# Units of the first token group in another order, nine idle products inside the first scores, first wides behind chunk 1

## The chip, the cores and the metric

The kernel runs on one core of one Trainium2 chip. TensorE (PE), VectorE (DVE), ScalarE (ACT), GpSimd (POOL) and SyncE (SP, here only a queue that issues DMAs) each work through their own instructions in order and wait for one another by semaphores. The metric is the device time of one execution in microseconds. The kernel before has a median of 972.02 us over 3 runs (971.38 to 975.17).

## The reference, cut to what matters

Three layers run one behind the other: a gated linear attention, a bilinear layer, and a mixture of eight experts of which each token takes two.

```python
for t in range(S):                                   # B=4, H=8, S=768, D=48
    state = alpha[:, :, t, :, None] * state + np.einsum('bhd,bhe->bhde', k[:, :, t], v[:, :, t])
    y[:, :, t] = np.einsum('bhd,bhde->bhe', q[:, :, t], state)
x = y.transpose(0, 2, 1, 3).reshape(3072, 384)
a = x @ w1;  b = x @ w2                              # 384 -> 1024
x = ((a * b) @ w3) @ w_out                           # 1024 -> 1024 -> 384
top2 = the two greatest of x @ w_gate + log1p(exp(x @ w_noise)) * noise
out[mask] += top2_w * (np.maximum(x[mask] @ e_w1[e], 0) @ e_w2[e])   # for each of 8 experts
```

The weights of the bilinear layer arrive as 64-bit floats, which the kernel converts itself. The large products run on pairs of 16-bit halves, three products for one.

## The kernel before, in words

The 3072 tokens are cut into eight groups of 384, each group into three chunks of 128 tokens. The attention works chunk by chunk: `prep_decay` and `prep_qk` (per pair of heads) turn alpha, q and k so that heads lie along the partitions and scale q and k by running products of alpha; `scores` (chunk j) multiplies them, copies the result out of PSUM (ACT, then a mask on POOL, for the first three chunks; DVE for the others); `ktok` turns k back; `mix` adds what the carried state gives and the scores times v, takes the greatest exponent of the result (a square on ACT, three short steps on DVE) and splits it into two 16-bit halves (ACT the high one, DVE the low one); `state` updates the carried state, which the next chunk's `mix` needs; `xturn` turns the split output into `xT`, copied out by ACT (L396). With `xT` of a group, `wide` forms a tile of `a` or `b` (nine products of 128 weights by the group's tokens), and `narrow` the product with the fused w3·w_out.

In the first 110 us there is a second stream of work: the weights of the bilinear layer are converted by `to_float32` and `split`, one block of 128 rows at a time, 36 blocks. Each costs DVE a shift (L410), ACT a copy of 16-bit words (L411), DVE a merge (L412), ACT the high half (L174) and DVE the low half (L178).

PE's instructions stand in the order in which the program is written (`manual_schedule`); those of DVE, ACT, POOL and SP are put in order by a scheduler, which works from its own costs. The writing is done by the loop at the end of `body`: it draws units from `att_units`, each with a cost, and until the third chunk of the first group is turned (`MS = 2`) it follows each unit either by a `wide` on the first chunk's 128 tokens (once chunk 0 is turned and six of the blocks are converted) or by three products of no use on a tile of zeros (`warm`, 128x512, L1161). Behind that point it interleaves units of attention with `mix_units` (the wides on the remaining 256 tokens, then full groups, then `narrow`) by a running sum of costs. `fetch` on SP's queue reads the weight blocks; its last four reads before `load(1)`, which reads alpha, q, k, v of the second group, wait until blocks 3 to 6 are converted, since they reuse their rooms.

Of the kernel before, what the change touches and what calls it, by code (L numbers as in the profile page):

```python
# [19 lines left out]
B, H, S, D = 4, 8, 768, 48  # L20
P = 128
# [4 lines left out]
NK = DM // P  # L26
# [16 lines left out]
RF = 5  # L43
RG = 6
WB = 12
WU = 3
WP = 3
TA = 30
CS = 1.5
# [29 lines left out]
def body(ctx, tc, q, k, v, alpha, mw1, mw2, mw3, mwo, wg, wn, noise, ew1, ew2, out, dbg=None):  # L79
# [208 lines left out]
    def scores(j):  # L288
        r, cols = cut(j)
        scs = [bank(NP, P) for _ in range(2)]  # L290
        for h in range(H):
            rows = slice(64 * (h % 2), 64 * (h % 2) + D)
            nc.tensor.matmul(scs[h % 2][:, h // 2, :], r["Kt"][rows, h // 2, cols], r["Qt"][rows, h // 2, cols],
                             start=True, stop=True)
        SM[j] = []
        for s in range(2):
            if j // TG in SCL:
                sf = late.tile([P, NP, P], F32, name="sf")
                sm = late.tile([P, 2, NP, P], F16, name="sm16", bufs=4)
                nc.vector.tensor_tensor(sf, scs[s], CSL[j // TG][:, None, :].to_broadcast([P, NP, P]), OP.mult)  # L300
                split(sf, sm[:, 0], sm[:, 1], engine=nc.gpsimd)
                SM[j].append(sm)
                continue
            sm = ap_.tile([P, NP, P], F32, name="sm", bufs=3)
            if j in AFF:
                nc.scalar.activation(sm, scs[s], AF.Copy)
                nc.gpsimd.affine_select(out=sm, in_=sm, pattern=[[0, NP], [1, P]], compare_op=OP.is_ge, fill=0.0,
                                        base=0, channel_multiplier=-1)
            else:
                nc.vector.tensor_tensor(sm, scs[s], causal[:, None, :].to_broadcast([P, NP, P]), OP.mult)  # L310
            SM[j].append(sm)
        if j // TG in SCL:
            VH[j] = late.tile([P, 2, H, D], F16, name="vh")
            split(VT[j], VH[j][:, 0], VH[j][:, 1], SCL[j // TG][:, 1:2])
# [74 lines left out]
    def xturn(j):  # L389
        ys = YS.pop(j)  # L390
        if j % TG == 0:
            XT[j // TG] = xp.tile([P, 2 * NK, G], F16, name="xT")
        xt = bank(2 * NK, P, dt=F16)
        for kk in range(2 * NK):
            nc.tensor.transpose(xt[:, kk, :], ys[:, kk // NK, kk % NK * P:(kk % NK + 1) * P], ident16)
        nc.scalar.activation(XT[j // TG][:, :, j % TG * P:(j % TG + 1) * P], xt, AF.Copy)  # L396
# [38 lines left out]
    nconv = 0  # L435
# [80 lines left out]
    def wide(g, f, i, c1=G):  # L516

        xT = XT[g]
        fs = slice(f * P, (f + 1) * P)
        c0 = GS.get((g, f, i), 0)  # L520
        GS[g, f, i] = c1
        cs, n = slice(c0, c1), c1 - c0
        pm = bank(n)
        for kk in range(NK):
            nc.tensor.matmul(pm, wab[i][0][:, kk, fs], xT[:, kk, cs], start=kk == 0, stop=False)  # L525
            nc.tensor.matmul(pm, wab[i][0][:, kk, fs], xT[:, NK + kk, cs], start=False, stop=False)  # L526
            nc.tensor.matmul(pm, wab[i][1][:, kk, fs], xT[:, kk, cs], start=False, stop=kk == NK - 1)  # L527
        a = gp.tile([P, G], F32, name=f"ab{i}")[:, :n]
        nc.scalar.activation(a, pm, AF.Copy, scale=SG if i == 0 else 1.0)  # L529
        AB[i] = a  # L530
        if i:
            a = AB[0]
            nc.vector.tensor_tensor(a, AB[1], a, OP.mult)
            if c0 == 0:
                GS[g, f] = [gp.tile([P, G], F16, name=x, bufs=10) for x in ("gh", "gl")]
            gh, gl = GS[g, f]
            split(a, gh[:, cs], gl[:, cs], engine=nc.gpsimd if g == 0 and f in PGL else None)
# [151 lines left out]
    def unit(c, f, *a):  # L689
        return c, (lambda: f(*a))  # L690

    def att_units():
        yield unit(0.0, prep_open, 0)
        for pr in range(NP):
            yield unit(0.33, prep_decay, 0, pr)
            if pr:
                yield unit(0.66, prep_qk, 0, pr - 1)
        yield unit(0.66, prep_qk, 0, NP - 1)
        yield unit(1.7, scores, 0)
        yield unit(0.44, ktok, 0)  # L700
        yield unit(1.7, scores, 1)
        yield unit(2.55, mix, 0)
        yield unit(0.44, ktok, 1)
        yield unit(0.75, state, 0)
        yield 0.34, (lambda: (xturn(0), done.add(0)))
        yield unit(0.0, loads_of_1)
        yield unit(1.7, scores, 2)
        yield unit(2.55, mix, 1)
        yield unit(0.44, ktok, 2)
        yield unit(0.75, state, 1)  # L710
        yield 0.34, (lambda: (xturn(1), done.add(1)))
        yield unit(0.0, prep_open, 1)
        yield unit(0.0, norms, 1)
        yield unit(0.33, prep_decay, 1, 0)
        yield unit(2.55, mix, 2)
        yield unit(0.33, prep_decay, 1, 1)
        yield 0.34, (lambda: (xturn(2), done.add(2)))
        yield unit(0.66, prep_qk, 1, 0)
        yield unit(0.33, prep_decay, 1, 2)
        yield unit(0.66, prep_qk, 1, 1)  # L720
        yield unit(0.33, prep_decay, 1, 3)
        yield unit(0.66, prep_qk, 1, 2)
        yield unit(0.66, prep_qk, 1, 3)
        yield unit(0.0, scales_of, 1)
        yield unit(0.0, load, 2)
        yield unit(0.0, tables)
        yield unit(0.75, state, 2)
        yield unit(1.7, scores, 3)
        yield unit(0.44, ktok, 3)
        for j in range(TG, NG * TG):  # L730
            st, cc = divmod(j, TG)
            more = st + 1 < NG
            if j + 1 < NG * TG:
                yield unit(1.7, scores, j + 1)
            if more and cc == 0:
                yield unit(0.0, prep_open, st + 1)
                yield unit(0.0, norms, st + 1)
                yield unit(0.33, prep_decay, st + 1, 0)
                yield unit(0.33, prep_decay, st + 1, 1)
            yield unit(2.55, mix, j)  # L740
            if more and cc == 0:
                yield unit(0.66, prep_qk, st + 1, 0)
                yield unit(0.33, prep_decay, st + 1, 2)
            if more and cc == 1:
                yield unit(0.66, prep_qk, st + 1, 2)
            if j + 1 < NG * TG:
                yield unit(0.44, ktok, j + 1)
            yield unit(0.75, state, j)
            if more and cc == 0:
                yield unit(0.66, prep_qk, st + 1, 1)  # L750
                yield unit(0.33, prep_decay, st + 1, 3)
            if more and cc == 1:
                yield unit(0.66, prep_qk, st + 1, 3)
                yield unit(0.0, scales_of, st + 1)
                if st + 2 < NG:
                    yield unit(0.0, load, st + 2)
            yield 0.34, (lambda j=j: (xturn(j), done.add(j)))
# [405 lines left out]
    done, ready = set(), set()  # L1163
# [3 lines left out]
    with tc.manual_schedule(engines={mybir.EngineType.PE}):  # L1167
        M = iter(mix_units())
        nxt = next(M)
        ta = tm = t0 = 0.0  # L1170
        warm(WB)
        for c, f in att_units():
            turned = set(done)
            f()
            ready |= turned
            ta += c
            if MS not in done:
                t0 = ta
                dve = [i for i in nc.cur_bb.bb.instructions[-40:] if i.engine == mybir.EngineType.DVE]
                marks += dve[-1:]  # L1180
                if marks:
                    with tc.issue_after(marks[max(0, len(marks) - LAG)]):
                        convert(int(CR * (ta - CS)))
                if c and 0 in done and nconv >= 2 * NK and pieces:
                    wide(0, *pieces.pop(0), P)
                elif c:
                    warm(WP if ta < 4.1 else WU)
                continue
            while nxt is not None and nxt[2] in ready | {0} and tm < RATIO * (min(ta, TK) - t0) + R2 * max(ta - TK, 0.0):
                nxt[1]()  # L1190
                tm += nxt[0]
                nxt = next(M, None)
        att.close()
        open_experts()
        early = iter(EARLY)
        while nxt is not None:
            nxt[1]()
            if nxt[0]:
                prepare(next(early, 1))
            nxt = next(M, None)  # L1200
        li = experts()
# [33 lines left out]
```

## Time and profile before

| | us |
|---|---|
| median of 3 runs | 972.02 |
| profiled execution, own time | 978.31 |
| its span, first to last instruction | 976.6 |
| PE busy in the span | 924.2 |
| DVE busy | 616.1 |
| ACT busy | 457.8 |
| mean granted clock of TensorE | 0.973 |

The profiled execution lies 6.3 us above the median. A row of the timeline gives the start, the busy time, the engine, the line and the operation with output and inputs, its shape and count; in brackets stands how long the engine sat idle before it and what ended that. A row of a window gives its length, then for PE, weight loads, DVE, ACT and POOL the busy time and count, then the granted clock as a share of 2.4 GHz, and the DMA share. Float32 products count twice (x16 for eight). A busy time of one row can overlap the start of the next by about 0.1 us.

### The profile page before, as it was taken

Reading aid. Unit: us, or ns where it says so; the run is one execution under the profiler, and the core shown is the slowest. Engines: PE = TensorE matmul, PEld = TensorE weight load, DVE = VectorE, ACT = ScalarE, POOL = GpSimd, SP = SyncE. Lnnn points to the kernel's source line nnn. Section 1 sums busy time; section 2 is a strip of 40 time slices with the busy share of each in tenths; the row PEclk is TensorE's granted clock in tenths of the full one; section 3 lists DMA queues with packets and bytes.
Section 4 is the critical chain, followed back from the end, with each engine's and each line's share of the span. In section 5 each row is a group of like instructions: output and inputs, shape, how many; then the busy total and the mean of one; then the engine's idle time right before and its main releaser. Section 6 shows DMA issues by size and latency. Waiting matters only on the chain. (4 is left out here: it accounts for less than half of the span.)

```text
span 976.6 us, 17652 instructions
## 1 busy us (share of the span) xinstructions
PE 924.2 (95%) x6823; PEld 607.8 (62%) x6823; DVE 616.1 (63%) x1697; ACT 457.8 (47%) x916; POOL 254.0 (26%) x246
## 2 busy tenths in 40 slices
PE   7889999999899998999999989999999999999996
PEld 4777777777666675666655445654656565656564
DVE  6698878576778697686768736626354454545320
ACT  3876665363565746555446424324243343334321
POOL 1121110004041311204052061433333333333313
PEclk9798899999999999999999989999999999999998
DMA  9886571334805224000234264874658575656313
GB/s 242 224 163 109 162 195 53 63 52 145 187 3 96 27 66 58 25 2 26 68 102 127 87 129 139 138 174 104 167 89 163 102 178 118 161 124 157 41 13 46
DMA packets 189269, 105.54 MB, mean 108 GB/s; under 512 B 156912, under 2 KB 174912, under 8 KB 189184
## 3 DMA queue, kind: packets, MB, share of 16 engines
q1 hardware_dynamic: 172624, 68.04, 31.5%
q0 software_dynamic: 16560, 36.37, 17.3%
q8 instruction: 54, 0.88, 0.4%
q14 instruction: 31, 0.25, 0.1%
HBM read 73.06 MB, written 20.31 MB: 96 GB/s over the span
## 5 line engine op out<-in xcount | busy, mean ns | idle before, releaser
L904 DVE SCALAR_TENSOR_TENSOR hl<-ps,hh 128x512 f16<-128x512 f32 (+1 forms) x128 | 74.9, 587 | 110.9 <-ACT hh L903 110.9
L934 POOL DMA_INDIRECT out_dram<-ysb,mt x56 | 88.3, 1576 | 210.3 <-ACT ysb L933 91.3
L900 PE MATMUL ps<-xT,eh 128*128 128x320 f16 (+1 forms) x384 | 132.0, 344 | 4.5 <-DMA xT<-xg 4.5
L901 PE MATMUL ps<-xT,eh 128*128 128x320 f16 (+1 forms) x384 | 131.9, 344 | 0.0
L902 PE MATMUL ps<-xT,el 128*128 128x320 f16 (+1 forms) x384 | 131.7, 343 | 0.0
L912 PE MATMUL ps<-eh,hl 128*128 128x384 f16 x384 | 125.2, 326 | 0.0
L911 PE MATMUL ps<-el,hh 128*128 128x384 f16 x384 | 125.2, 326 | 0.0
L910 PE MATMUL ps<-eh,hh 128*128 128x384 f16 x384 | 125.2, 326 | 0.0
L903 ACT ACTIVATE hh<-ps 128x512 f16<-128x512 f32 (+1 forms) x128 | 65.9, 516 | 113.6 <-PE ps L902 112.5
L933 ACT ACTIVATE ysb<-ps,wv 128x384 f32<-128x384 f32 (+1 forms) x56 | 32.5, 580 | 151.9 <-PE ps L912 75.2
L178 DVE SCALAR_TENSOR_TENSOR el<-es,esc,eh 128x512 f16<-128x512 f32 (+1 forms) x80 | 67.0, 856 | 46.4 <-ACT eh L174 45.1
L679 POOL DMA_INDIRECT table<-md,ad x48 | 49.3, 1028 | 162.7 <-DVE ad L676 130.4
L888 POOL DMA_INDIRECT xg<-x2s,mt x56 | 56.4, 1008 | 57.8 <-DMA mt<-table 37.6
L176 POOL TENSOR_TENSOR sm<-sf,sm 128x512 f16<-128x512 f32 x24 | 28.4, 1203 | 161.1 <-ACT sm L174 161.1
L529 ACT ACTIVATE ab<-ps 128x384 f32<-128x384 f32 (+2 forms) x136 | 61.4, 465 | 17.0 <-PE ps L527 15.5
L525 PE MATMUL ps<-xT,w1h 128*128 128x384 f16 (+2 forms) x204 | 65.7, 323 | 2.0 <-ACT ab L529 1.5
L525 PE MATMUL ps<-xT,w0h 128*128 128x384 f16 (+2 forms) x204 | 65.4, 322 | 1.1 <-ACT xT L396 1.1
L549 PE MATMUL ps<-Wh,gh 128*128 128x400 f16 x192 | 63.9, 333 | 2.2 <-ACT gh L174 2.2
L527 PE MATMUL ps<-xT,w1l 128*128 128x384 f16 (+2 forms) x204 | 65.8, 323 | 0.0
L526 PE MATMUL ps<-xT,w1h 128*128 128x384 f16 (+2 forms) x204 | 65.7, 323 | 0.0
L526 PE MATMUL ps<-xT,w0h 128*128 128x384 f16 (+2 forms) x204 | 65.4, 322 | 0.0
L527 PE MATMUL ps<-xT,w0l 128*128 128x384 f16 (+2 forms) x204 | 65.3, 321 | 0.0
(285 smaller groups left out, 2080.6 us busy)
## 6 DMA issues: line engine op xcount, KB each, us to landing
es<-in_moe_w_dram SPq DMA_DIRECT2D x32, 768.0 KB, 4.8
s<-in_moe_w_dram POOLq DMA_DIRECT2D x16, 512.0 KB, 4.3
out_dram<-zero POOLq DMA_DIRECT2D x5, 960.0 KB, 9.4
v<-in_v_dram SPq DMA_DIRECT2D x24, 192.0 KB, 3.6
x2s<-xr SPq DMA_DIRECT2D x24, 192.0 KB, 1.9
pad<-in_alpha_dram SPq DMA_DIRECT2D x21, 192.0 KB, 4.3
pad<-in_q_dram SPq DMA_DIRECT2D x21, 192.0 KB, 4.8
pad<-in_k_dram SPq DMA_DIRECT2D x21, 192.0 KB, 5.0
```

Of the source, the lines that this page charges most:

```text
L178: nc.vector.scalar_tensor_tensor(lo, src, scale, hi, op0=OP.mult, op1=OP.subtract)
L525: nc.tensor.matmul(pm, wab[i][0][:, kk, fs], xT[:, kk, cs], start=kk == 0, stop=False)
L526: nc.tensor.matmul(pm, wab[i][0][:, kk, fs], xT[:, NK + kk, cs], start=False, stop=False)
L527: nc.tensor.matmul(pm, wab[i][1][:, kk, fs], xT[:, kk, cs], start=False, stop=kk == NK - 1)
L900: nc.tensor.matmul(pm, w1h[:, kk, fs], xT[:, kk, :n], start=kk == 0, stop=False)
L901: nc.tensor.matmul(pm, w1h[:, kk, fs], xT[:, NK + kk, :n], start=False, stop=False)
L902: nc.tensor.matmul(pm, w1l[:, kk, fs], xT[:, kk, :n], start=False, stop=kk == NK - 1)
L904: nc.vector.scalar_tensor_tensor(hl[:, f], pm, 0.0, hh[:, f], op0=OP.max, op1=OP.subtract)
L910: nc.tensor.matmul(py[:n], hh[:, f, ts], w2h[:, f], start=f == 0, stop=False)
L911: nc.tensor.matmul(py[:n], hh[:, f, ts], w2l[:, f], start=False, stop=False)
L912: nc.tensor.matmul(py[:n], hl[:, f, ts], w2h[:, f], start=False, stop=f == NF - 1)
L934: i = queued(lambda: nc.gpsimd.indirect_dma_start(out=out, out_offset=bass.IndirectOffsetOnAxis(ap=mt[:n, t, 0:1].bitcast(U32), axis=0), i ...
```

## The change

The units of the first three chunks are written in another order (`scores` of chunk 1 and both `ktok` before the first `mix`, `scores` of chunk 2 before the first `xturn`, two more units of the second group's preparation before the third `xturn`). Three products of no use follow only the units of the preparation (cost sum under 4.1). Nine of them stand inside the scores of chunk 0, ahead of the last two heads. The eight wides on the first chunk come in pairs, from the turn of chunk 1 on.

```diff
-WU = 3
+W0 = 9
...
         for h in range(H):
             rows = slice(64 * (h % 2), 64 * (h % 2) + D)
+            if j == 0 and h == H - 2:
+                warm(W0)
             nc.tensor.matmul(scs[h % 2][:, h // 2, :], r["Kt"][rows, h // 2, cols], r["Qt"][rows, h // 2, cols],
...
         yield unit(1.7, scores, 0)
+        yield unit(1.7, scores, 1)
         yield unit(0.44, ktok, 0)
-        yield unit(1.7, scores, 1)
+        yield unit(0.44, ktok, 1)
         yield unit(2.55, mix, 0)
-        yield unit(0.44, ktok, 1)
         yield unit(0.75, state, 0)
+        yield unit(1.7, scores, 2)
         yield 0.34, (lambda: (xturn(0), done.add(0)))
         yield unit(0.0, loads_of_1)
-        yield unit(1.7, scores, 2)
         yield unit(2.55, mix, 1)
...
         yield unit(0.33, prep_decay, 1, 0)
+        yield unit(0.33, prep_decay, 1, 1)
         yield unit(2.55, mix, 2)
-        yield unit(0.33, prep_decay, 1, 1)
+        yield unit(0.66, prep_qk, 1, 0)
         yield 0.34, (lambda: (xturn(2), done.add(2)))
-        yield unit(0.66, prep_qk, 1, 0)
...
-                if c and 0 in done and nconv >= 2 * NK and pieces:
-                    wide(0, *pieces.pop(0), P)
-                elif c:
-                    warm(WP if ta < 4.1 else WU)
+                if c and ta < 4.1:
+                    warm(WP)
+                elif c and 1 in done:
+                    for piece in pieces[:2]:
+                        wide(0, *piece, P)
+                    del pieces[:2]
                 continue
```

In the changed program lines behind the scores stand two lower (L411 is L413, L529 is L531). On PE, behind the preparation of the first group, a piece of the program before reads as follows: `mix` of chunk 0, three useless products (each with its weight load), `ktok` of chunk 1.

```order
L343 MATMUL ps<-v,sm 128x48 x8
L1161 LDWEIGHTS ident_67
L1161 MATMUL ps<-idle,ident_67 128x512
L1161 LDWEIGHTS ident_67
L1161 MATMUL ps<-idle,ident_67 128x512
L1161 LDWEIGHTS ident_67
L1161 MATMUL ps<-idle,ident_67 128x512
L322 MATMUL ps<-ident,Kt 128x128 x4
```

In the changed program PE has there, from the last of the nine products inside the scores on (L295 is scores, L324 ktok, L345 mix, L364 state, L397 xturn):

```order
L1163 LDWEIGHTS ident_67
L1163 MATMUL ps<-idle,ident_67 128x512
L295 MATMUL ps<-Qt,Kt 128x128 x10
L324 MATMUL ps<-ident,Kt 128x128 x8
L345 MATMUL ps<-v,sm 128x48 x8
L364 MATMUL ps<-v,ks 112x96 x4
L295 MATMUL ps<-Qt,Kt 128x128 x8
L397 LDWEIGHTS ys
L397 MATMUL ps<-ident_67,ys 128x128
```

The scores of chunk 2 stand ahead of the turn of chunk 0, no useless product is left between these units, and the 21 that stood behind the preparation (seven triples) are replaced by the nine.

On ACT, at the first scores, before: the word copy of a block (L411), its high half (L174), the two copies of the scores (L306), two more word copies with `ktok`'s copy between them.

```order
L411 ACTIVATE w1h<-w1h 128x512
L174 ACTIVATE w0h<-s_319 128x512
L306 ACTIVATE sm<-ps 128x512 x2
L411 ACTIVATE w1l<-w1l 128x512
L324 ACTIVATE ks<-ps 128x512
L411 ACTIVATE x_142<-x_142 128x512
```

In the changed program:

```order
L413 ACTIVATE w1h<-w1h 128x512
L174 ACTIVATE w0h<-s_319 128x512
L413 ACTIVATE w1l<-w1l 128x512
L413 ACTIVATE x_142<-x_142 128x512
L308 ACTIVATE sm<-ps 128x512 x2
L174 ACTIVATE w0h<-s_369 128x512
```

Both word copies have moved ahead of the copies of the first scores.

On ACT, at the third chunk of the first group, before (L350 is the square that follows `mix` of chunk 2, L529 takes a wide out of PSUM, L222 the turned alpha, `gh` is the high half of a product `a*b`, the last row the copy of the turned chunk into `xT`):

```order
L174 ACTIVATE gh<-ab_648 128x128
L411 ACTIVATE s_145<-s_145 128x512
L174 ACTIVATE w1h<-s_632 128x512
L350 ACTIVATE ys,xsc<-ps 128x384
L411 ACTIVATE xT<-xT 128x384
L529 ACTIVATE ab_749<-ps 128x128
L222 ACTIVATE A_760<-ps 128x3x128
L174 ACTIVATE ys<-ps,xsc 128x384
L174 ACTIVATE w1h<-s_727 128x512
L396 ACTIVATE xT<-ps 128x6x128
```

In the changed program (L352 is the square, L398 the copy):

```order
L174 ACTIVATE gh<-ab_676 128x128
L352 ACTIVATE ys,xsc<-ps 128x384
L531 ACTIVATE ab_738<-ps 128x128
L413 ACTIVATE s_145<-s_145 128x512
L413 ACTIVATE xT<-xT 128x384
L174 ACTIVATE ys<-ps,xsc 128x384
L174 ACTIVATE w1h<-s_716 128x512
L174 ACTIVATE woh<-s_722 128x384
L531 ACTIVATE ab_750<-ps 128x128
L413 ACTIVATE xT<-xT 128x384
L398 ACTIVATE xT<-ps 128x6x128
```

The square stands right behind a high half of the third product `a*b`; between it and the copy there are three word copies instead of one. That product is made on DVE, and DVE's order before it has both preparations of the second group's first two pairs:

```order
L229 SCALAR_TENSOR_TENSOR Gx<-A_611,Bend 128x384
L228 MEMSET A_655 128x4
L230 RECIPROCAL Bst_117<-Gx 128x3
L232 TENSOR_TENSOR Ae<-sm_615,Gx 128x3
L229 SCALAR_TENSOR_TENSOR Gx<-A_655,Bend 128x384
L231 SCALAR_TENSOR_TENSOR A<-A_611,Bst_117 128x384
L230 RECIPROCAL Bst_118<-Gx 128x3
L232 TENSOR_TENSOR Ae<-sm_659,Gx 128x3
L535 TENSOR_TENSOR ab_676<-ab_688,ab_676 128x128
```

Before, the third such product stood ahead of the first step of such a preparation (L227):

```order
L373 TENSOR_TENSOR Zs_119<-ps,Zs_120 48x4x48
L410 TENSOR_SCALAR s_632<-s_144 128x512
L374 TENSOR_TENSOR Zs_119<-Zs_119,Ae 48x4x48
L533 TENSOR_TENSOR ab_648<-ab_668,ab_648 128x128
L227 COPY sm_687<-A_683 128x3
```

Three scans (L229, L231) have moved ahead of a product for which ACT's queue waits.

## Rows read from the trace of the kernel before

**Rows 1.** Page, busy us of each engine, share of the span, instructions
```profile
PE 924.2 (95%) x6823; PEld 607.8 (62%) x6823; DVE 616.1 (63%) x1697; ACT 457.8 (47%) x916; POOL 254.0 (26%) x246
```

**Rows 2.** Windows: length, busy us (count) of PE, PEld, DVE, ACT, POOL; clock; DMA
```profile
25.00:50.00 25.00, 22.13 (x161) 19.02 (x160) 16.38 (x33) 20.26 (x34) 4.04 (x8) 0.71 0.83 218
50.00:75.00 25.00, 20.28 (x187) 17.37 (x184) 24.17 (x60) 17.53 (x38) 5.35 (x8) 0.93 0.92 163
...
23.30:53.10 29.80, 25.92 (x196) 21.89 (x194) 19.50 (x41) 25.06 (x45) 6.32 (x11) 0.73 0.89 221
53.10:75.30 22.20, 18.18 (x152) 15.46 (x152) 21.41 (x54) 14.43 (x30) 4.16 (x6) 0.92 0.88 160
```

**Rows 3.** Windows cut where the granted clock changes, and one stretch of full clock
```profile
22.30:25.60 3.30, 3.18 (x12) 1.95 (x13) 1.06 (x4) 2.35 (x4) 1.22 (x2) 0.50 1.09 343
...
36.00:49.50 13.50, 12.97 (x86) 12.49 (x86) 7.38 (x17) 8.76 (x16) 1.82 (x3) 0.50 0.74 151
...
56.50:59.70 3.20, 3.20 (x17) 2.06 (x17) 2.87 (x10) 2.73 (x7) 0.00 (x0) 0.50 1.03 249
...
77.00:83.60 6.60, 6.60 (x40) 5.66 (x39) 5.66 (x14) 4.40 (x10) 0.67 (x1) 0.50 0.77 87
83.70:110.90 27.20, 26.35 (x221) 21.74 (x218) 25.05 (x68) 21.06 (x46) 3.66 (x7) 1.00 0.46 121
```

**Rows 4.** Timeline of PE at the second group's first scores: start, busy, count [idle before]
```profile
75.38 0.49 PE L293 MATMUL ps<-Qt,Kt 48*128 48x128 f32 x4 [0.65 <-DVE Kt L240]
```

**Rows 5.** Timeline of PE through the first group
```profile
22.42 0.80 PE L293 MATMUL ps<-Qt,Kt 48*128 48x128 f32 x4 [3.18 <-DVE Qt L240]
...
27.95 1.88 PE L343 MATMUL ps<-v,sm 128*128 128x48 f32 x16
...
31.40 0.94 PE L362 MATMUL ps<-v,ks 128*112 128x96 f32 x8
...
37.58 2.08 PE L293 MATMUL ps<-Qt,Kt 48*128 48x128 f32 x16
...
42.29 3.54 PE L343 MATMUL ps<-v,sm 128*128 128x48 f32 x16
...
46.58 1.06 PE L322 MATMUL ps<-ident,Kt 128*128 128x128 f32 x4
...
48.40 1.52 PE L362 MATMUL ps<-v,ks 128*112 128x96 f32 x8
...
50.26 0.50 PE L395 MATMUL ps<-ident,ys 128*128 128x128 f16 x6
...
53.87 1.10 PE L332 MATMUL ps<-Zs,Qt 112*128 112x96 f32 x8 [1.78 <-DVE Zs L374]
...
61.61 0.27 PE L525 MATMUL ps<-xT,w0h 128*128 128x256 f16 x1 [0.24 <-ACT xT L396]
```

**Rows 6.** Windows of the useless products alone (L1161): busy (count) of PE, PEld; clock
```profile
23.10:34.00 10.90, 5.72 (x18) 1.78 (x18) 0.88 1.01 324
58.30:60.00 1.70, 1.49 (x3) 0.30 (x2) 0.57 1.03 298
```

**Rows 7.** Timeline of ACT through the first group
```profile
23.25 1.09 ACT L306 ACTIVATE sm<-ps 128x512 f32<-128x512 f32 x2 [2.97 <-PE ps L293]
...
45.50 0.60 ACT L306 ACTIVATE sm<-ps 128x512 f32<-128x512 f32 x1 [3.54 <-PE ps L343]
...
56.97 0.49 ACT L350 ACTIVATE ys<-ps 128x384 f16<-128x384 f32 x1 [0.48 <-PE ps L343]
...
60.75 0.81 ACT L396 ACTIVATE xT<-ps 128x768 f16<-128x768 f16 x1 [0.57 <-PE ps L395]
```

**Rows 8.** Groups of ACT, 22 to 62 us: count, busy us, mean ns
```profile
L411 ACT ACTIVATE s<-s 128x512 uint16<-128x512 uint16 x3 | 4.0, 1342 | 0.0
```

**Rows 9.** Groups of DVE, 23.3 to 75.3 us
```profile
L229 DVE TENSOR_TENSOR_SCAN Gx<-A,Bend 128x384 f32<-128x384 f32 x4 | 4.2, 1040 | 0.0
```

**Rows 10.** Timeline of SP's queue: first read of the second group
```profile
40.43 3.62 SPq L186 DMA_DIRECT2D pad<-in_alpha_dram  x3
```

## The prediction

> **What bounds the kernel now.** I read the page first, then windows over the span, then windows cut where the clock changes, then the timelines of PE, ACT and DVE side by side for the first 110 us. PE is busy 95% of the span [rows 1], so time is won only where PE idles, runs slowly or does useless work. The change touches the first group, and there PE is not alone: from 25 to 50 us it is busy 22.13 of 25 at a mean clock of 0.71, ACT 20.26; from 50 to 75 PE is busy 20.28 and DVE 24.17 [rows 2]. The reader is to see three things. The chain of scores, mask, mix, square, split and turn runs through four engines, each of which also converts weights in between. PE is at half clock from 22.3 to 25.6, 36 to 49.5 and 56.5 to 59.7 [rows 3], each time after a gap or after short products. And the stage ends on DVE: the second group's first scores wait for the scaled q and k, the last of them until 75.38 [rows 4], while DVE has been busy 21.41 of 22.2 us [rows 2]. Behind them PE runs 77 to 83.6 at half clock without a gap, then is busy 26.35 of 27.2 us at full clock, DVE 25.05 [rows 3]. So three things decide: when DVE has that last k, how much PE has done by then, and at which clock PE goes on.
>
> **The change part by part.** All times are of the profiled execution, 978.31 us (span 976.6), which lies 6.29 above the median of 972.02; differences are carried over to the median as they are.
>
> *Nine products inside the scores.* Before the last two heads PE waits 3.18 us for q [rows 5]. Eighteen such products took 5.72 us, the first of them at half clock [rows 6], so nine take at most 2.9: they end before 22.42 and cost nothing. If that gap shrank below 2.9 they would cost the rest. They buy full clock from 22.42 on, where 22.3 to 25.6 stood at half [rows 3]; the four products that end the scores take 0.4 instead of 0.8.
>
> *Seven triples go.* Six of them (5.72 us busy) stood between 23.1 and 34, one (1.49) at 58.3 [rows 6]. Little of it is on the path, because something else is late next. On ACT two word copies (1.34 each, some 1.2 from start to start [rows 8]) now stand ahead of the copies of the first scores, which started at 23.25 [rows 7]; these start near 25.0, end near 26.1, and with the masks `mix` 0 can start near 27.2 instead of 27.95 [rows 5]. Of 5.72 us, 0.75 are left.
>
> *Scores of chunk 2 ahead of the turn of chunk 0.* `state` 0 waits for the copy behind `ktok` until near 29.4 (before 31.40); scores 2 follow and end near 33 instead of 39.66 (37.58 + 2.08) [rows 5]. But ACT's next instruction is the copy of those scores, and the high half for turn 0 stands behind it, so that turn stays near 35. `mix` 1 follows at once, without the scores and the wides that stood between: it ends near 40.3 instead of 45.83, `ktok` 2 and `state` 1 (1.06 and 1.52) bring PE to 42.8 instead of 49.92, and turn 1, which waits for ACT and DVE, ends near 46.3 instead of 50.76 [rows 5]. ACT's wait of 3.54 us for `mix` 1 [rows 7] shrinks to 0.8, but DVE now waits about 2.5 for `state` 1.
>
> *The clock from 27 to 46.* The trace of before does not show it for this order: there triples filled the time to 33. Bounds: all at full clock, or all at half, as 36 to 49.5 was although PE was busy 12.97 of 13.5 us [rows 3]. I take half: what stands there now is the work of 36 to 49.5, short products, with waits between. The times above are at half from `state` 0 on.
>
> *Eight wides behind chunk 1.* They are no new work. Their copies out of PSUM stand on ACT behind three word copies (3 x 1.2) and two high halves, so the first is out near 51.6. With eight PSUM banks in turn `mix` 2 needs the bank of the first wide: start near 52 instead of 53.87 [rows 5]. Of 4.5 us of lead, under 2 are left.
>
> *The third chunk.* The square behind `mix` 2 stands on ACT behind a high half that waits for a product on DVE, and DVE now has three scans (1.04 each [rows 9]) and their small steps ahead of that product, some 3.9 us from the first product `a*b` (near 53.4): 57.3. Before, from the square at 56.97 to the end of the turned copy at 61.56 (60.75 + 0.81) [rows 7] 4.6 us passed; now there are two more word copies (1.2 and, with fewer columns, 0.8) and 0.1 of small ones, and the wait of 0.57 is gone, 6 us in all. So `xT` is complete near 63.2 and the wides on the other 256 tokens, first at 61.61 [rows 5], begin 1.6 us later. PE idles most of 57 to 62.
>
> *DVE to the last k.* By the order it has the same work up to there plus one low half, about 0.5 us. Its idle time from 23.3 to 53.1, wait by wait in the new order, comes to 10.7 us, against 29.8 - 19.5 = 10.3 before [rows 2]: +0.4. Behind 53.1 it idled 22.2 - 21.41 = 0.8 [rows 2]; now it waits for the late chunk (0.7) and for turns that stand on PE behind the late wides (0.3 if these run at full clock, 1.9 at half): +0.2 to +1.8. Sum +1.1 to +2.7; I take +1.6, nearer to full clock, since wides are dense.
>
> *PE behind it.* Scores 3 end 1.6 later, and a wide (nine products, 0.98 us at full clock by the starts behind 61.61 [rows 5]) that stood ahead of them stands behind: +1.0. Against it, 77 to 83.6 need not be at half clock, since PE's long pause now lies before 63: of 6.6 us [rows 3] up to 3.3 come back. Bounds 0 and -3.3; I take all, as the pause that preceded that stretch is the one that moves. DVE's own lag of 1.6 has room: it idles 27.2 - 25.05 = 2.15 us in 83.7 to 110.9 [rows 3].
>
> *The rest.* SP's reads of the second group, from 40.43 [rows 10], wait for a merge on DVE that comes about 2 us earlier; PE turns the first of them behind 47, so they stay hidden. From then on attention stands one unit ahead of the wides; nothing is added or dropped.
>
> Sum: +1.6 + 1.0 - 3.3 = -0.7, and 972.0 - 0.7 = 971.3 us.
>
> **The rivals.**
> *The clock stays up (faster).* At full clock from 27 to 46 `mix` 1 takes half of its 3.54 us [rows 5] and turn 1 ends near 42. DVE's waits for `state` 0 and 1 fall by about 3.3, smaller ones by 0.8, so the last k comes 1.6 - 4.1 = -2.5; with the wide and the clock -2.5 + 1.0 - 3.3 = -4.8: 967.2. For it: the nine products close the gap that led to half clock at 22.3. Against it: in 36 to 49.5 short products without a break did not bring the clock back.
> The Trainium skill (TensorE: Matmul & The Clock Gate, Terms) prices time at half clock at that time multiplied by one minus the ratio. By that rule alone the three stretches before 60 [rows 3], 3.3 + 13.5 + 3.2 = 20.0 us, would give back 10.0: 962.0. The trace bears it out where PE has no waits, as in 77 to 83.6; in 25 to 50 ACT, busy 20.26 of 25 [rows 2], takes over, so I count this as the tail of the rival.
>
> *The third chunk holds everything up (slower).* One mechanism: ACT's high half waits behind DVE's scans, `xT` of chunk 2 comes late, PE pauses from 57 on, starts the wides at half clock and makes DVE wait for the turns between them. With +2.7 at the last k, 0.8 more of pause before it, the wide's +1.0 and no clock regained: +4.5, 976.5. It decides from the point where that copy ends after 64. For it: 6 us of ACT rows in between. Against it: DVE, which bounds the stage, goes on converting.
>
> *The order changes nothing that lasts.* DVE was busy 24.17 of 25 us [rows 2] and keeps its work; what the chain wins the conversions take, and the half clock comes back behind the second group's first scores with part of the lag made up: 972.0 to 973.5.
>
> **How the numbers follow.** About 0.5% (4.9 us) is what a measurement of this kernel can tell from no change: below 967.2 is faster, above 976.9 slower. Chances: forecast 0.42, clock up 0.24, third chunk 0.19, nothing that lasts 0.15. The fast rival lies on the bound, half of it beyond (0.12), and the forecast's tail adds 0.08; of the slow one somewhat under half is beyond (0.09), with 0.05 from the others. So faster 0.2, same 0.66, slower 0.14. The range takes in both rivals' prices: 966 to 977.5.
>
> **What would show it.** In the changed profile: full clock from 22 to 25; `mix` 0 within half a microsecond of 27.2; turn 1 ending between 45 and 48 (near 42: the clock stayed up); `mix` 2 near 52; the third copy into `xT` ending near 63; the first scores of the second group ending near 77.5, and full clock behind them. I am wrong if the third copy ends before 60 or after 64, or if DVE idles less than 8 us between 23 and 53.

## The result and the profile after

The change makes the kernel slower. Its median is 986.11 us over 4 runs (984.76 to 989.23), that of before 973.6 in the same comparison (971.38 to 981.9); the ratio is 1.0109, 95% interval 1.0081 to 1.0137. A ratio here is taken over the fast runs of both kernels and need not be the quotient of the two medians. The forecast was 971.3, with 966 to 977.5 as its range.

The profiled executions differ by less, 984.76 against 978.31, because that of before lost time in a place far behind the change. One window of each, of the same work in the experts (columns as in [rows 2]), before and then after:

```profile
650.00:680.00 30.00, 27.30 (x201) 14.93 (x200) 13.38 (x24) 10.29 (x20) 11.88 (x9) 0.94 0.50 97
```

```profile
657.00:687.00 30.00, 29.84 (x229) 17.25 (x228) 15.11 (x27) 11.77 (x22) 10.51 (x8) 1.00 0.64 127
```

Before idled 2.7 of these 30 us and ran part of them at a lower clock, after did neither. When each product of the one trace is paired with the same product of the other, after is 0.4 us early at 94 us, 1.2 late at 120 to 126, and then, on the products of the wides and narrows, 3.9 at 144, 6.6 at 225, 9.9 at 282, 12.2 at 498 (pairs near one time differ by up to 5 us there, since the orders differ). It is still 11 us at 600, and 4.4 of it go where before stalled. So in this trace the first group, the part that was rewritten, ends within 1.2 us of before, and some 11 us arise between 120 and 500 us, where the diff changes no line.

The page's busy times, against [rows 1], show that no work was added: PE has twelve products fewer, 21 useless ones replaced by nine, and is busy as long.

```profile
PE 925.0 (94%) x6811; PEld 608.0 (62%) x6811; DVE 619.2 (63%) x1697; ACT 460.2 (47%) x916; POOL 256.7 (26%) x246
```

Now the first group. PE's timeline of after, to be held against [rows 4, 5]; behind the scores lines stand two lower than before:

```profile
22.18 1.39 PE L295 MATMUL ps<-Qt,Kt 48*128 48x128 f32 x20 [1.21 <-DVE Qt L240]
...
27.69 2.52 PE L345 MATMUL ps<-v,sm 128*128 128x48 f32 x14 [0.94 <-POOL sm L309]
30.02 1.77 PE L364 MATMUL ps<-v,ks 128*112 128x96 f32 x8
31.72 2.08 PE L295 MATMUL ps<-Qt,Kt 48*128 48x128 f32 x16
...
37.72 3.54 PE L345 MATMUL ps<-v,sm 128*128 128x48 f32 x16
...
46.92 0.50 PE L397 MATMUL ps<-ident,ys 128*128 128x128 f16 x3 [0.57 <-DVE ys L178]
...
53.37 1.08 PE L334 MATMUL ps<-Zs,Qt 112*128 112x96 f32 x8
...
62.56 0.48 PE L397 MATMUL ps<-ident,ys 128*128 128x128 f16 x3 [4.70 <-ACT ys L174]
...
65.23 0.37 PE L527 MATMUL ps<-xT,w0h 128*128 128x256 f16 x1 [0.67 <-ACT xT L398]
...
75.67 0.94 PE L295 MATMUL ps<-Qt,Kt 48*128 48x128 f32 x12
77.25 0.49 PE L295 MATMUL ps<-Qt,Kt 48*128 48x128 f32 x4 [0.65 <-DVE Qt L240]
```

The reader is to see how close the walk through the group came. Turn 1 ends at 47.42 instead of 50.76. The third turn then waits 4.70 us, which it did not before, and the wides behind it start at 65.23 instead of 61.61. The second group's first scores end at 77.74; the working had 77.5.

Windows of after, to be held against [rows 2, 3]:

```profile
22.30:25.60 3.30, 2.29 (x28) 1.93 (x28) 2.13 (x5) 3.12 (x4) 0.10 (x1) 1.00 1.09 344
28.50:52.40 23.90, 19.73 (x124) 18.38 (x124) 15.10 (x34) 18.18 (x29) 2.73 (x5) 0.50 0.95 198
52.40:62.60 10.20, 5.50 (x68) 5.27 (x67) 9.20 (x27) 6.96 (x20) 3.79 (x6) 1.00 0.78 183
62.60:69.40 6.80, 5.75 (x29) 4.34 (x30) 5.45 (x13) 4.07 (x9) 1.01 (x2) 0.50 0.20 60
...
23.30:53.10 29.80, 22.94 (x158) 21.11 (x155) 19.03 (x39) 24.08 (x38) 6.06 (x10) 0.60 0.97 219
```

The nine products keep the clock up at 22.3, but behind 28.5 it is at half for 23.9 us without a break, where before had 13.7. PE idles 4.7 of the 10.2 us from 52.4 on and then runs 6.8 us at half clock.

### The profile page after: what moved, and what is told of

Its sections match the earlier page's. It is cut to its first block, busy times and chain, and to the rows that moved or that the text cites. A ratio compares the mean times of both kernels' runs of the same rounds, so it can differ in the third digit from the quotient of the medians.

```text
span 983.0 us, 17620 instructions
## 1 busy us (share of the span) xinstructions
PE 925.0 (94%) x6811; PEld 608.0 (62%) x6811; DVE 619.2 (63%) x1697; ACT 460.2 (47%) x916; POOL 256.7 (26%) x246
## 4 chain that ended last, share of the span: by engine, by line
PE 55%; DVE 23%; ACT 7%; issue 6%; DMA 4%; SPq 2%; POOL 1%; POOLq 0%; ACTq 0%; DVEq 0%
PE ps L912 6%; PE ps L914 6%; PE ps L913 6%; PE ps L902 5%; PE ps L904 5%; PE ps L903 5%; PE ps L553 2%; DVE esc L861 2%; PE ps L551 2%; PE ps L527 2%; DVE ab L535 2%; PE ps L552 2%; PE ps L529 2%; PE ps L528 2%; PE ps L345 2%
## 5 line engine op out<-in xcount | busy, mean ns | idle before, releaser
L531 ACT ACTIVATE ab<-ps 128x384 f32<-128x384 f32 (+2 forms) x136 | 61.6, 465 | 16.6 <-PE ps L529 14.7
L527 PE MATMUL ps<-xT,w0h 128*128 128x384 f16 (+2 forms) x204 | 66.5, 327 | 1.5 <-ACT xT L398 0.7
L528 PE MATMUL ps<-xT,w0h 128*128 128x384 f16 (+2 forms) x204 | 66.4, 326 | 0.0
L529 PE MATMUL ps<-xT,w0l 128*128 128x384 f16 (+2 forms) x204 | 66.3, 326 | 0.0
L529 PE MATMUL ps<-xT,w1l 128*128 128x384 f16 (+2 forms) x204 | 65.7, 323 | 0.0
```

## The experiments

The running sum of costs decides how many wides stand between the units of attention. It starts at `t0`, the attention's sum at the third turn (`tm < RATIO * (ta - t0)`, with `RATIO` 2). The change puts one more unit, `prep_qk(1, 0)` of cost 0.66, ahead of that turn. So `t0` is 0.66 higher, and from there to the end of attention the wides stand 1.32 of cost later; one full wide counts 1.48. Medians below are in us, of the kernel and of the kernel before measured beside it (973.6 to 980.18, so only ratios compare across experiments), and the ratio has its 95% interval.

**The new group with the old pacing.** Built on the kernel after:

```diff
-                t0 = ta
+                t0 = ta - 0.66
```

> The changed kernel with one number set back: the running sum that decides how far the wides follow attention starts 0.66 lower, as before, so that behind the third turn TensorE's instructions stand exactly as in the kernel before. Theory A (the lag of one unit behind the first group costs the time; the new first group itself costs about 2 us): 2 to 4 us above before, ratio near 1.003. Theory B (the new first group delays conversions, and the delay grows later): as slow as the changed kernel, 10 to 12 us above before, ratio 1.010 or more. Theory C (half clock falls by chance in later groups): anything between, and a spread of several us over the runs.

Measured: 981.78 against 980.18, ratio 1.0021 (0.9992 to 1.0050). Behind the third turn PE's order is now that of before, and most of the loss is gone. What is left lies in the first group: paired with before's, every product of this trace is 2.8 to 2.9 us late from 123 to 250 us.

**The old group with the new pacing.** Built on the kernel before:

```diff
-                t0 = ta
+                t0 = ta + 0.66
```

> The kernel before with that running sum started 0.66 higher, so that behind the third turn TensorE's instructions stand as in the changed kernel, while the first group is untouched. Theory A: 7 to 10 us above before, ratio near 1.009. Theory B: within 1 us of before. Theory C: anything between, with a wide spread.

Measured: 988.16 against 980.18, ratio 1.0084 (1.0051 to 1.0118). No unit of the first group is moved, and three quarters of the loss are there. The two ratios add to 1.0105, where the whole change has 1.0109: the pacing is the cause of most of the loss, and the group's own part is at most the half per cent that the first interval leaves.

One place is the second group's first scores. PE's timeline, before and then this kernel:

```profile
69.91 0.49 PE L467 MATMUL ps<-ident,s 128*128 128x128 f32 x3
70.23 0.27 PE L525 MATMUL ps<-xT,w1h 128*128 128x256 f16 x1
...
72.39 0.72 PE L293 MATMUL ps<-Qt,Kt 48*128 48x128 f32 x8 [1.01 <-DVE Qt L240]
74.24 0.49 PE L293 MATMUL ps<-Qt,Kt 48*128 48x128 f32 x4 [1.13 <-DVE Kt L240]
```

```profile
68.25 0.49 PE L467 MATMUL ps<-ident,s 128*128 128x128 f32 x3
68.67 0.94 PE L293 MATMUL ps<-Qt,Kt 48*128 48x128 f32 x12
72.94 0.80 PE L293 MATMUL ps<-Qt,Kt 48*128 48x128 f32 x4 [3.33 <-DVE Qt L240]
```

Before, the second half of a wide stands between the small transposes and the scores; now the scores come straight on and PE waits 3.33 us in one piece for DVE. The total there differs little (before 1.01 + 1.13 + 0.65 = 2.79, with [rows 4]). The rest comes later. PE's waits by what ended them (total, times, longest), over the same stretch of work, before (60 to 506 us) and then this kernel (59 to 513):

```profile
PE ps L293 <- DVE Kt L240: 6.7, 7, 2.0
PE ps L549 <- ACT gh L174: 2.2, 2, 1.5
...
PE ps L293 <- DVE Qt L240: 1.0, 1, 1.0
```

```profile
PE ps L293 <- DVE Kt L240: 5.7, 5, 1.8
PE ps L293 <- DVE Qt L240: 4.3, 2, 3.3
PE ps L549 <- ACT gh L174: 4.2, 4, 1.7
PE ps L293 <- ACT ab L529: 1.8, 1, 1.8
PE ps L497 <- DVE w3l L178: 1.6, 2, 0.8
```

The scores wait more for q and for a copy on ACT, `narrow` (L549) more for a high half, the fused weights (L497) more for a conversion: all waits of the stretch sum to 19.4 us (21 waits) before and 24.2 (23 waits) here. From the third copy into `xT` to the narrows of the seventh group this trace takes 9.9 us longer than before's; PE idles 5.2 of them more, and 6.8 us more stand at half clock, worth up to 3.4 (half of it, where PE does not wait). After has the same picture: its scores wait 1.8 on ACT's copy, its `narrow` 4.1 in 4 waits.

**Where along the way.** The lag only in the early part, built on before with `t0 = ta + 0.66`, and only in the late part, built on before alone with `- (1.32 if ta > 54 else 0.0)` at the same place:

```diff
-            while nxt is not None and nxt[2] in ready | {0} and tm < RATIO * (min(ta, TK) - t0) + R2 * max(ta - TK, 0.0):
+            while nxt is not None and nxt[2] in ready | {0} and tm < RATIO * (min(ta, TK) - t0) + R2 * max(ta - TK, 0.0) + (1.32 if ta > 54 else 0.0):
```

> The kernel before with the wides one unit behind only until about 160 us, where the order of before is restored. If the lag costs evenly wherever attention waits for DVE: 3 to 5 us of the 8 of the second experiment, ratio 1.003 to 1.005. If only the later groups pay: within 1 us of before.

> The counterpart: the order of before until about 160 us, the wides one unit behind from there on. If the lag costs evenly: 3 to 5 us, ratio 1.003 to 1.005, and with the first part 8 together. If only the early part pays: within 1 us of before.

Measured: early lag 986.77 against 979.21, 1.0072 (1.0048 to 1.0097); late lag 981.12, 1.0024 (0.9994 to 1.0054). They add to 1.0096, near the 1.0084 of the whole lag. Three quarters arise before 160 us, so the cost is not even; whether the late part costs anything is open, since its interval includes 1. PE's timeline in the early-lag kernel, its waits:

```profile
72.34 0.80 PE L293 MATMUL ps<-Qt,Kt 48*128 48x128 f32 x4 [3.30 <-DVE Qt L240]
...
105.43 1.16 PE L293 MATMUL ps<-Qt,Kt 48*128 48x128 f32 x14 [0.97 <-DVE Qt L240]
...
160.49 0.34 PE L497 MATMUL ps<-woh,w3l 128*128 128x400 f16 x1 [0.80 <-DVE w3l L178]
163.93 0.34 PE L497 MATMUL ps<-woh,w3l 128*128 128x400 f16 x1 [0.81 <-DVE w3l L178]
```

The last three are not in before's trace; the third group's first scores, at 134, wait 1.67 where they waited 0.65. Together PE idles 3.6 us more from the third copy into `xT` to the first group's narrows, and the work there takes 4.4 longer. DVE still splits weights in this stretch, as the last two waits show; that it is therefore late for the scores, and that each wide that stood in front was cover, is a reading of these waits.

The waits go with the pacing in all fourteen traces of this record. After, like the early-lag kernel, waits at the second group's last scores and at the third group's first; before waits only at the latter, and less (its row stands behind those of after):

```profile
107.92 1.16 PE L295 MATMUL ps<-Qt,Kt 48*128 48x128 f32 x14 [0.97 <-DVE Qt L240]
136.07 0.49 PE L295 MATMUL ps<-Qt,Kt 48*128 48x128 f32 x4 [1.67 <-DVE Kt L240]
```

```profile
134.27 0.49 PE L293 MATMUL ps<-Qt,Kt 48*128 48x128 f32 x4 [0.65 <-DVE Kt L240]
```

The wait at the second group's last scores is 0.97 or 0.98 us in the four traces that lag early (after, early lag, the old group with the new pacing, and the kernel of the next experiment) and absent in the other ten. The fifth group's first scores wait 3.51 to 4.27 us in the three that lag there and keep the order of scores (after, late lag, the old group with the new pacing), and 0.33 to 2.00 in the ten that do not lag there. From the third copy to the last narrow the four that lag early take 488.4 to 492.8 us, of which PE idles 26.0 on the mean; the eight with before's pacing take 477.4 to 487.3 and idle 21.6. The means lie 8.0 us apart: 4.4 of it are idle time, and 5.3 us more at half clock are worth up to 2.7.

**First scores later.** The waits ahead of the first scores suggest that it is enough to move these. The edit does so from the third group on; the second group's, with the 3.33 us, stay where they were. Built on the old group with the new pacing:

```diff
-            if j + 1 < NG * TG:
+            if j + 1 < NG * TG and cc < TG - 1:
...
+            if j + 1 < NG * TG and cc == TG - 1:
+                yield unit(1.7, scores, j + 1)
```

> The second experiment (old first group, wides one unit behind) with one more edit: the first scores of every group from the third on stand behind the mix of the chunk ahead instead of before it. If the lag costs because those scores reach TensorE before DVE has scaled q and k: TensorE's waits for Kt and Qt behind 130 us fall from about 7 us to under 3, and the ratio falls from 1.008 to 1.001 to 1.004. If it costs by other waits (narrow for the last high half, half clock): it stays at 1.007 or more.

Measured: 985.01 against 975.98, 1.0083 (1.0057 to 1.0110). That idea fell. Behind 130 us the scores no longer wait for k or q (5.7 us in the old group with the new pacing), but the ratio stays. The wait went elsewhere; PE's waits from 60 to 520 us:

```profile
PE ps L332 <- DVE Zs L374: 5.5, 2, 4.2
PE ps L549 <- ACT gh L174: 5.3, 4, 1.8
```

The product with the carried state (L332) now waits up to 4.2 us for DVE's state. So it is not the place of the scores that costs: PE waits for DVE and ACT at the next place that needs them.

**More wides than before.** If cover helps, one wide more might help further. Built on after:

```diff
-                t0 = ta
+                t0 = ta - 1.32
```

> The changed kernel with the running sum started 1.32 lower: the wides stand nearly one unit further ahead of attention than before. Theory A, if the cost is monotone in the lag: at or below the first experiment, up to 4 us below before. Theory A, if before merely stood at a good place: a few us above the first experiment. Theory B: 986.

Measured: 991.98 against 980.18, 1.0114 (1.0065 to 1.0162). It is not monotone: 10.2 us above the new group with the old pacing, where a few had been expected at most. The waits from 60 to 520 us:

```profile
PE ps L527 <- ACT ab L531: 5.1, 2, 4.0
PE ps L397 <- ACT ys L174: 5.0, 1, 5.0
```

Now the wides themselves wait for ACT to copy a wide out of PSUM, up to 4.0 us. (The second row is the third turn's wait, which after has as well.)

**The third chunk's tail put back.** Built on after; the two units stand where they stood, and the pacing is then before's by itself:

```diff
-        yield unit(0.33, prep_decay, 1, 1)
         yield unit(2.55, mix, 2)
-        yield unit(0.66, prep_qk, 1, 0)
+        yield unit(0.33, prep_decay, 1, 1)
         yield 0.34, (lambda: (xturn(2), done.add(2)))
+        yield unit(0.66, prep_qk, 1, 0)
```

> The changed kernel with its last piece put back: the second preparation of alpha stands behind the mix of chunk 2 and the first of q and k behind the third turn, as before; with that the wides lag as before, too. Theory A with the third step of the prediction (two preparations ahead of ACT's high half make the third turn late): the third copy into xT ends near 60 to 61 instead of 64.3 to 66.3, and the time is 2 to 4 us below the first experiment (ratio 0.995 to 1.000). Rival (the third copy is late because of the wides behind chunk 1): it stays near 64 and the ratio near 1.002.

Measured: 976.63 against 975.98, 0.9995 (0.9971 to 1.0019). ACT's timeline, of after and then of this kernel:

```profile
58.62 0.31 ACT L174 ACTIVATE gh<-ab 128x128 f16<-128x128 f32 x1 [1.82 <-DVE ab L535]
58.83 0.47 ACT L352 ACTIVATE ys<-ps 128x384 f16<-128x384 f32 x1
...
61.08 1.11 ACT L413 ACTIVATE xT<-xT 128x384 uint16<-128x384 uint16 x1
...
64.28 0.90 ACT L398 ACTIVATE xT<-ps 128x768 f16<-128x768 f16 x1
```

```profile
56.32 0.57 ACT L352 ACTIVATE ys<-ps 128x384 f16<-128x384 f32 x1
...
61.32 0.81 ACT L398 ACTIVATE xT<-ps 128x768 f16<-128x768 f16 x1
```

In after the square (L352) waits behind a high half for a product on DVE, and the copy (L398) starts 3.0 us later than with the tail put back, and 5.0 later in the new group with the old pacing (66.3), which is the same program up to there; turn 1 is alike here (its last products at 46.92 and 46.87). So the third chunk is held up as the second rival had it. What that costs at the end isn't settled: this kernel lies 0.26% below the new group with the old pacing, and the intervals overlap.

**Nine products alone**, built on before, and measured a second time:

```diff
+            if j == 0 and h == H - 2:
+                warm(9)
```

> The kernel before with the nine products inside the first scores and nothing else. All theories expect full clock from 22 to 25 us and no change beyond 1 us: the products fill a wait, and DVE and ACT bound the stage. If the time falls by more than 2 us, the clock of the first scores was worth more than the prediction said.

> The nine products alone once more, beside the others: ratio 0.995 to 0.998 if the gain of 3.7 us is real, 0.999 or more if it was chance.

Measured: 975.69 against 980.18, 0.9962 (0.9933 to 0.9991), and 976.26 against 979.21, 0.9975 (0.9946 to 1.0003). This part of the change, alone, has the lowest ratios measured, 3 to 4.5 us below before by the medians; the first interval excludes 1, the second just includes it. The expectation missed, since it allowed no change beyond 1 us. The gain is not at the wait itself: the products behind it start at 22.30 and 23.12 in the two traces, 22.42 before. But the third copy into `xT` starts at 56.40 and 56.93 instead of 60.75 [rows 7]:

```profile
56.40 0.81 ACT L398 ACTIVATE xT<-ps 128x768 f16<-128x768 f16 x1 [0.42 <-PE ps L397]
```

Up to there 6.8 us stand at half clock in both traces, 20.5 before, and from 135 to 225 us every product is 4.9 and 6.6 us earlier than before's. That the clock is what gains this is likely but not shown by a run of its own.

**Nine products, no triples behind the preparation.** Built on the former:

```diff
-                    warm(WP if ta < 4.1 else WU)
+                    warm(WP if ta < 4.1 else 0)
```

> The kernel before with the nine products inside the first scores and without the seven triples between the units. If the triples only fill PE where ACT and DVE bound the stage: within 1.5 us of the nine alone (ratio 0.995 to 0.998). If they keep the clock up for the mixes and scores: half clock from about 28 on, and 2 to 5 us slower than the nine alone.

Measured: 975.37 against 975.98, 0.9998 (0.9970 to 1.0027). The trace looks like the second case of the expectation: half clock from 26.2 for 27.3 us, the third copy at 63.56 instead of 56.40, and every product from 135 to 240 us 4.0 later than with the triples. The ratios, 0.9962 and 0.9975 with triples, point the same way, but the intervals overlap.

**Tail put back, triples put back**, built on the kernel with the tail put back:

```diff
+                elif c:
+                    warm(WP)
```

> The changed kernel with its tail put back and with the triples kept behind the units until the turn of chunk 1 (the new order of scores, ktok and mixes, the nine products, the wides in pairs, and triples). If the triples earn their place by keeping the clock up: full clock through most of 25 to 45, the second turn near 43 to 44 instead of 47.5, and 2 to 4 us below the tail alone (ratio 0.991 to 0.997). If they only take TensorE's time: at or above the tail alone (0.9995).

Measured: 977.39 against 979.21, 0.9983 (0.9957 to 1.0009). The clock and the chain are seen side by side. One window of each, with the tail put back without triples and then with them:

```profile
27.00:45.00 18.00, 14.27 (x82) 13.17 (x81) 11.45 (x26) 14.28 (x24) 4.02 (x6) 0.57 0.78 228
```

```profile
27.30:47.80 20.50, 17.12 (x142) 12.64 (x141) 15.66 (x31) 19.16 (x30) 4.68 (x8) 1.00 0.83 219
```

And the end of turn 1, in the same two kernels:

```profile
46.87 0.50 PE L397 MATMUL ps<-ident,ys 128*128 128x128 f16 x3 [0.57 <-DVE ys L178]
```

```profile
46.78 0.34 PE L397 MATMUL ps<-ident,ys 128*128 128x128 f16 x3 [0.78 <-DVE ys L178]
```

Triples bring the clock from a mean of 0.57 to 1.00, and turn 1 moves by 0.1 us: DVE's low half releases it in both, and ACT is busy 19.16 of those 20.5 us. Behind turn 1 the triples gain more: the third copy into `xT` starts at 59.2 instead of 61.32, and from 126 to 250 us every product is 0.8 us earlier. The Trainium skill (TensorE: Matmul & The Clock Gate, Terms) prices time at half clock at that time multiplied by one minus the ratio; for the 18.0 us at 0.57 that is an estimate of 7.7 us. The traces do not agree here: 0.1 us at turn 1, 2.1 at the third copy and 0.8 behind it are less, and the two ratios to before, 0.9995 and 0.9983, lie within each other's intervals. In the old order, where wides stand one by one, the triples gain more in the traces (4.0 us, above).

**Wides one by one behind chunk 0**, as before, in the kernel with the tail put back:

```diff
-                elif c and 1 in done:
-                    for piece in pieces[:2]:
-                        wide(0, *piece, P)
-                    del pieces[:2]
+                elif c and 0 in done and nconv >= 2 * NK and pieces:
+                    wide(0, *pieces.pop(0), P)
```

> The tail put back and, besides, the eight wides one by one from the turn of chunk 0 on, as before: of the change there remain the order of scores, ktok and the first mixes, the nine products and the missing triples. If placing the wides in pairs behind chunk 1 costs by their late copies on ACT: 1 to 3 us below the tail alone. If not: the same as the tail alone.

Measured: 983.76 against 975.98, 1.0074 (1.0050 to 1.0098). The expectation missed: in this order, wides in pairs behind chunk 1 are worth 7.1 us (983.76 - 976.63). Turn 1's products start at 52.69 instead of 45.80; early wides now stand ahead of the chain on PE and ACT, and the clock is at half from 24.9 for 27.3 us and again from 59.0 for 13.7.

## Why the prediction was wrong

Point by point, by its own steps:

- *Nine products.* Right: they fill the wait for q (1.21 us are left of it), the clock is full from 22 to 25, and they cost nothing. Alone they are most likely a gain, which the sum had only as part of its clock.
- *Seven triples, scores of chunk 2.* Right within 1.1: the rest of `mix` 0 starts at 27.69 (27.2), scores 2 end at 33.80 (33), turn 1 at 47.42 (46.3).
- *The clock from 27 to 46.* Half was taken, half it was, and it went on to 52.4. The first rival, in which the clock stays up, so fell on its premise. It had turn 1 some 4 us earlier at full clock; with triples the clock was full and turn 1 moved by 0.1, so its price is not borne out either, as far as products of no use can stand for it.
- *Eight wides.* `mix` 2 starts at 53.37 (52), 1.4 late: of the 2 us of lead that were left, 0.5 are.
- *The third chunk.* The mechanism is right and shown by putting the tail back; the copy ends at 65.18 where 63.2 stood in the sum. The prediction itself said that it is wrong if that is after 64. Of the 2 us that were missing, 1.5 are the square's, which starts at 58.83 (57.3) behind DVE's scans, and 0.4 the rows behind it, 6.35 us from its start to the end of the copy (6).
- *DVE to the last k, PE behind it.* Idle from 23.3 to 53.1 is 29.8 - 19.03 = 10.8 (10.7). Scores 3 end at 77.74 (77.5), and the clock is full from 69.4 to 110.4, though 62.6 to 69.4 took its place at half. At 94 us the paired products are 0.4 early; the sum said 0.7. It fits its terms: 1.9 late at the last scores, with the sum's 1.0 for the wide and 3.3 back from the clock, gives 0.4 early.
- *The rest.* This is the step that failed: "From then on attention stands one unit ahead of the wides; nothing is added or dropped", priced at nothing. The +1.0 for one wide was charged once, at the second group's first scores, and the same shift behind them was taken as free because the work stays the same. But PE keeps its order, and with one wide less ahead of a unit it waits longer for DVE and ACT: 0.97 us instead of none at the second group's last scores, 1.67 instead of 0.65 at the third group's first, 3.5 to 4.3 instead of at most 2.0 at the fifth group's first, and more ahead of `narrow`. The old group with the new pacing loses 0.84% by this alone.

In after's trace, from the fourth copy into `xT` (109.3 us) to the narrows of the last group, the loss of 10.2 us is 3.7 of PE's idle time and 10.2 us more at half clock, worth up to 5.1. Of that half clock 6.8 us stand at 264, behind the waits of the fifth group's first scores (1.80, 0.86 and 1.54). Before's profiled execution had full clock there, but it is alone in that: the thirteen other traces have 3.4 to 10.2 us at half clock that begin between 248 and 268, and the seven with the old pacing among them 3.4 to 6.8. So most of this part is the luck of the execution of before that was profiled, not the lag. Open is why before's place is better than its neighbours on both sides: one wide less makes PE wait for DVE, one more for ACT's copies, but no run here separates what fixes the optimum.

The chance of slower, 0.14, was counted in the first group alone. No case of the prediction had its place behind 110 us. With the pacing put right the ratios are 1.0021 and 0.9995; their intervals hold the forecast (971.3 of 972.0, 0.9993) as well as the third rival, an order that changes nothing that lasts (1.000 to 1.0015), so no run decides between these two.

## What to carry to other kernels

Where a running sum of costs interleaves two streams on an engine that works in order, moving one unit across the sum's starting point shifts every later one: compare the whole order, and price the shift by the waits that the displaced work covered. Put such a starting point right again (one line here) before judging the rest of a change. And test a change's parts alone: the nine products were, in all likelihood, a gain inside a loss.

## What the runs showed that had not been expected

- A shift of 1.32 in the sum of costs, less than one wide (1.48), costs 0.84% one way in the old group; the other way, in the new group, it makes 1.0114 of 1.0021.
- TensorE stayed at half clock for 23.9 us in after, and with the tail put back full clock moved turn 1 by 0.1 us and the third copy by 2.1: in this chain the waits for ACT and DVE counted for more than PE's clock.
- The same first group stood at half clock for 13.7 us from 36 on in two traces (before, late lag) and for 3.4 from 37 or 38 on in two others (old group with the new pacing, early lag). One trace does not tell the clock of a stage.
- Nine idle products inside a wait gave 3 to 4.5 us by the medians, though the products behind the wait start no earlier (22.30 and 23.12, before 22.42).
